# First transfers of the last stage: one fixed order on the SyncE queue, and the last left rows turned on the ScalarE queue

## The chip, the cores and the metric

The kernel runs on one core of a Trainium2 chip. The metric is the device time of one execution in microseconds. TensorE is called PE here, VectorE DVE, ScalarE ACT, GpSimd POOL and SyncE SP. SP and ACT can each issue DMA transfers on a queue of their own (q1 and q10 in the profile), and POOL issues on a third (q0). All three are served by the same 16 DMA engines.

## The reference

The reference is the forward pass and all gradients of one block: a LayerNorm, a segment-recurrent attention (32 heads of 128, 64 segments of 32 rows, each with 8 memory rows that come out of the segment before), and a dense layer with a squared ReLU beside it.

```python
def _f(x, mem0, Wq, Wk, Wv, Wo, w1, b1, w2, b2):
    xn = layernorm(x)                                  # x: [1, 2048, 512]
    return x + attention(xn, mem0, Wq, Wk, Wv, Wo) + dense(xn, w1, b1, w2, b2)

# attention, for each of 64 segments s:
h = concatenate([mem, xn[:, 32*s:32*s + 32]])          # 8 + 32 rows
q, k, v = h @ Wq, h @ Wk, h @ Wv                       # 32 heads of 128
o = (softmax(mask(q @ k.T * scale)) @ v) @ Wo
mem, out = o[:, :8], o[:, 8:]

out, vjp = jax.vjp(_f, x, mem0, Wq, Wk, Wv, Wo, w1, b1, w2, b2)
return (out, *vjp(grad_out))
```

The last stage of the kernel makes the gradients of the four attention weights, each a product over all 2560 rows (2048 rows of the segments and 512 memory rows), and finishes the gradient of x.

## The kernel before

The kernel has four stages. The first is the dense layer, forward and backward. The second walks the 64 segments forward, the third walks them backward, in blocks of four segments (`NB` = 16 blocks), with orders of operations written out by hand. The fourth (the `p5` pools) computes the weight gradients; the change is at the border of the third and the fourth stage.

**End of the third stage.** The gradients of q, k and v of the segments' rows are stored to DRAM (`S_GB`, line L1154), those of the memory rows ("left rows") of each block are turned by a transposing DMA (L1187, tile `gNat`, source `b_gkL`, `b_gvL` or `b_gqL`) and then stored to `S_GL` (L1189). Both are issued on SP's queue. `gNat` has one buffer, so the three turns of a block follow each other, each after the store of the one before. Block 0 is the last block. Its turns come after the last matmul work of the stage. The sums of a block's left rows are stored to `S_XGL` (L1182), the gradient of the segments' inputs to `S_XG` (L1192). The gradient of the first memory goes out at the very end (`gm`, L1390, stored at L1391).

**The fourth stage.** There are 16 products, in the order of `COLS`: pairs (t, g) of a weight (3 is Wo, 2 Wv, 1 Wk, 0 Wq) and a quarter of the heads. Each product is eight accumulations of 20 matmuls, 160 in all (L1503). A product has two sides:

- The gradient rows `gn` (`rows_of`, tiles `gn5` in three pools, product i uses pool i % 3, `loads(i + 2)` is called at the start of product i). For t = 3 they are plain loads of S_ON and S_OL (L1419, L1425), for the first two products on POOL's queue. For the other t they are 16 turning transfers of S_GB on SP's queue (L1422) and four plain loads of S_GL (L1425), which need the turned left rows. gn0 and gn1 are plain, gn2 is turned.
- The fixed side, `GOc` for t = 3 and `HNc` (variable `side`) for the others, made once by `slot_side`: four turning transfers (L1407) and four plain copies (L1410), on ACT's queue. A matmul needs all four turns; the copies serve the last four of the 20 rows' groups.

The results leave through `leave`: ACT copies PSUM to `wt` (L1475, six buffers), POOL issues the store (L1476). After each product, `input_rows` finishes 128 rows of the gradient of x: POOL loads XT and XL (L1444, L1446) and three more tiles (L1449 to L1453), DVE merges XL into XT (L1447), PE turns XT into `ps_rows` (L1456), and DVE, ACT and POOL do the rest.

**What sets the order.** In the third stage and wherever `tc.manual_schedule()` is open, instructions stand in the order of the Python calls. Elsewhere a planner orders them by its own costs, engine by engine. The first transfers of the fourth stage are outside of such a block before:

```python
loads(0)
slot_side(GOc, S_GM, gflat)
loads(1)
slot_side(side, S_HT, S_XN[:])
```

Of the kernel before, what the change touches and what calls it, by code (L numbers as in the profile page):

```python
# [10 lines left out]
BF16 = mybir.dt.bfloat16  # L11
F32 = mybir.dt.float32
P = 128
# [13 lines left out]
def kernel(  # L27
# [27 lines left out]
    nc = tc.nc  # L55

    _, S, D = A_x.shape
    M = A_mem0.shape[1]
# [31 lines left out]
    gflat = grad_out.flatten_outer_dims()  # L90
# [5 lines left out]
    dma = nc.sync.dma_start  # L96
# [5 lines left out]
    NB = NSEG // SPB  # L102
    HG = 4
    KH = H // HG
# [10 lines left out]
    S_XN = dram.tile([S, D], BF16, name="S_XN")  # L115
    S_GT = dram.tile([P, DC, S], BF16, name="S_GT")

    S_HT = dram.tile([P, DC, S], BF16, name="S_HT")
    S_HX = dram.tile([S // P, P, DC, P], BF16, name="S_HX")
    S_XL = dram.tile([P, DC, S // SEG * M], BF16, name="S_XL")  # L120
    S_GM = dram.tile([P, DC, S], BF16, name="S_GM")
# [19 lines left out]
    S_GL = dram.tile([NB, HG, SEG, 3, GW], BF16, name="S_GL")  # L141
# [266 lines left out]
    def turned_heads(W):  # L408

        return lambda h: W[:, :, h * P:(h + 1) * P]  # L410
# [53 lines left out]
    def turn_ops(o, alloc, R4, st):  # L464

        def tT(c):
            if "T" not in st:
                st["T"] = alloc("ps_sum")
            nc.tensor.transpose(st["T"][:, c * P:(c + 1) * P], R4()[:, c * P:(c + 1) * P], identF[:])  # L469
        for h in range(2):  # L470
            o["t%s" % "ab"[h]] = lambda h=h: [tT(c) for c in (2 * h, 2 * h + 1)]

    def left_sums(XT, T):

        for c in range(DC):
            nc.vector.tensor_reduce(XT[:, c], T[:, c * P:(c + 1) * P].rearrange("p (g j t) -> p j t g", g=HG, j=SPB),
                                    axis=AX.X, op=ALU.add)
# [145 lines left out]
    with sb("fw", 1) as fw, psum("fr", 4) as fr, psum("fpp", 1) as fpp, \  # L623
# [26 lines left out]
        def big(name):  # L650
            return fr.tile([P, 512], F32, name=name, tag="r")
# [19 lines left out]
        def block(b):  # L671

            if b not in blk:
                shapes = {"kL": (fs, [P, KH, HG, NL], BF16), "OT": (fs, [P, HG, KH, SPB, SEG], BF16),
                          "X": (fs, [P, DC, P], BF16),
                          "kM": (fo, [P, KH, HG, NL], BF16), "vTM": (fo, [P, KH, HG, NL], BF16),
                          "XT": (fs, [P, DC, SPB, SEG], F32), "qL": (fo, [P, KH, HG, NL], BF16),
                          "VL": (fo, [P, GW], BF16), "vM": (fo, [P, GW], BF16), "EL": (fo, [P, KH, KW], BF16),
                          "OTL": (fo, [P, KH, HG, NL], BF16),
                          "bb": (fo, [P, D], BF16)}  # L680

                def make(n):
                    pool, shape, dt = shapes[n]
                    return pool.tile(shape, dt, name=n, tag=n)
                blk[b] = Tiles(make)
            return blk[b]
# [250 lines left out]
    with sb("la", 2) as la, sb("ls", 2) as ls, sb("lo", 1) as lo_, sb("wg", 2) as wg, psum("lpp", 1) as lpp, psum("lr", 4) as lr:  # L937
# [84 lines left out]
        side, part = {}, {}  # L1022
# [53 lines left out]
        with tc.manual_schedule():  # L1076
# [3 lines left out]
            for b in range(NB + 1):  # L1080
                for nm in LB_ORDER:
                    k = nm.rstrip("-")
                    c = b - (nm != k)
# [23 lines left out]
    with sb("bq", 1) as bq, sb("bt", 1) as bt, sb("bs", 2) as bs, sb("be", 1) as be, psum("bpp", 1) as bpp, psum("br", 4) as br:  # L1107
# [30 lines left out]
        def left(b):  # L1138
            B_ = block(b)
            ps, st, o = {}, {}, {}  # L1140
            src = {"v": "gvL", "k": "gkL", "q": "gqL"}
            o["lq"] = lambda: dma(B_["gqL"][:], S_GQL[b])

            def following(f):

                return lambda: f(b - 1) if b > 0 else None
            for n, f in loads.items():
                o[n] = following(f)
            o["gs"] = lambda: dma(S_GM[:, :, b * P:(b + 1) * P], gts[b][:])
            for t, n in enumerate("qkv"):  # L1150
                for x in range(2):
                    def so(n=n, t=t, gs=slice(2 * x, 2 * x + 2) if n == "v" else slice(0, HG),
                           ks=slice(0, KH) if n == "v" else HALF[x]):
                        dma(S_GB[b, t][:, gs, ks], G4[n][:, gs, ks].rearrange("p g k j r -> p g k (j r)"))  # L1154
                    o["%so%d" % (n, x)] = so

            jobs = [(turned_heads(Wqkv[t]), src[n], k) for t, n in ((2, "v"), (1, "k"), (0, "q")) for k in range(KH)]
            for i in range(4):
                for x, nm in enumerate("GHI"):
                    def G_(i=i, x=x):  # L1160
                        if ("R", i) not in ps:
                            ps["R", i] = big("ps_RL")
                            ps["n", i] = 0
                        ps["n", i] += 1
                        for m, (W, n, k) in enumerate(jobs[6 * i + 2 * x:6 * i + 2 * x + 2]):
                            for g in range(HG):
                                nc.tensor.matmul(ps["R", i][32 * g:32 * g + 32, :].rearrange("p (a b) -> p a b", b=P),  # L1167
                                                 lhsT=B_[n][:, k, g, :], rhs=W(g * KH + k), start=(ps["n", i] == 1 and m == 0),
                                                 stop=(ps["n", i] == 3 and m == 1), tile_position=(0, 32 * g))
                    o["%s%d" % (nm, i)] = G_  # L1170
                if i == 0:
                    o["ra0"] = lambda: ENGS["L.ra0"](B_["R4"][:], ps["R", 0][:])
                else:
                    o["ra%d" % i] = lambda i=i: nc.vector.tensor_tensor(out=B_["R4"][:], in0=ps["R", i][:],
                                                                        in1=B_["R4"][:], op=ALU.add)
            turn_ops(o, big, lambda: B_["R4"], st)

            def xt():
                st["XL"] = bt.tile([P, DC, SPB, M], F32, name="b_XL", tag="XL")
                left_sums(st["XL"], st["T"])  # L1180
            o["xt"] = xt
            o["sl"] = lambda: dma(S_XGL[b], st["XL"][:])  # L1182

            for t, n in enumerate("qkv"):
                def nt(n=n):
                    st[n] = bt.tile([P, KH, P], BF16, name="gNat", tag="gNat")
                    nc.sync.dma_start_transpose(st[n][:], B_[src[n]][:].rearrange("p k g r -> p k (g r)"))  # L1187
                o[n + "tr"] = nt
                o[n + "st"] = lambda n=n, t=t: dma(S_GL[b].rearrange("g r t c -> (g r) t c")[:, t, :],  # L1189
                                                   st[n][:].rearrange("p k e -> p (k e)"))  # L1190

            o["sx"] = lambda: dma(S_XG[b], B_["XT"][:].rearrange("p c j r -> p c (j r)"))  # L1192
            return o

        pre, gts, loads = {}, {}, {}
# [161 lines left out]
        with tc.manual_schedule():  # L1357
# [3 lines left out]
            for b in range(NB):  # L1361
                lefts.append(left(b))
# [34 lines left out]
    with sb("p5a", 1) as p5a, sb("p5h", 1) as p5h, sb("p5", 2) as p5, sb("p5g", 1) as p5g, \  # L1397
# [6 lines left out]

        def slot_side(t_, srcT, src):
            for dc in range(DC):
                nc.scalar.dma_start_transpose(t_[:, 0:NB, dc * P:(dc + 1) * P], srcT[:, dc, :])  # L1407
            lv = src.rearrange("(c q r) d -> c q r d", q=16, r=SEG)
            for c in range(NLC):
                nc.scalar.dma_start(t_[:, NB + c, :], lv[c][:, 0:M, :])  # L1410
            return t_

        def rows_of(i, g, blocks, left_):

            t_ = (p5a, p5b, p5c)[i % 3].tile([P, RC_ALL, CW], BF16, name="gn5", tag="gn%d" % (i % 3))
            q = pdma if i < 2 else dma
            if blocks is None:
                for b in range(NB - 4, -1, -4):
                    q(t_[:, b:b + 4, :], S_ON[b:b + 4, g].rearrange("b p c -> p b c"))  # L1419
            else:  # L1420
                for b in range(NB - 1, -1, -1):
                    nc.sync.dma_start_transpose(t_[:, b, :].rearrange("p (k e) -> p k e", k=KH),  # L1422
                                                blocks(b)[:, g].rearrange("p k r -> p (k r)"))
            for j in range(SPB):
                q(t_[32 * j:32 * j + 32, NB:RC_ALL, :], left_(g).rearrange("(c j) r x -> j r c x", j=SPB)[j])  # L1425
            return t_
# [6 lines left out]
        def loads(i):  # L1433
            if i < len(COLS):
                t, g = COLS[i]
                if t == 3:
                    got[i] = rows_of(i, g, None, lambda g: S_OL[:, g])
                else:
                    got[i] = rows_of(i, g, lambda b: S_GB[b, t], lambda g: S_GL[:, g, :, t, :])
# [40 lines left out]
        p5g.tile([P, 896], BF16, name="gap5")  # L1480
        GOc = p5g.tile([P, RC_ALL, D], BF16, name="GOc")
        side = p5h.tile([P, RC_ALL, D], BF16, name="HNc")
        loads(0)
        slot_side(GOc, S_GM, gflat)
        loads(1)
        slot_side(side, S_HT, S_XN[:])
        for i, (t, g) in enumerate(COLS):
            loads(i + 2)
            gn = got[i]
# [52 lines left out]
```

## Time and profile before

| | us |
|---|---|
| median of 3 runs (lowest, highest) | 3085.69 (3084.45, 3087.76) |
| the profiled execution, its own time | 3083.57 |
| its span, first to last instruction | 3081.8 |
| PE busy in the span | 2698.1 (88%) |
| DVE, ACT, POOL busy | 1332.6, 973.0, 659.1 |
| third stage's last matmul on PE ends at | 2431.8 |
| first matmul of the fourth stage, product 0 ends | 2508.3, 2544.5 |
| last matmul of the fourth stage ends at | 3069.0 |

A line of a group gives the line of the program, the engine, the operation, the tile written and the tiles read, the count, then busy time, mean nanoseconds of one, and the idle time just before them with what ended it. Engine names with a q (SPq, ACTq, POOLq) stand for DMA issues on that engine's queue. Times of the chain and of timelines are microseconds from the start of the span. The profile is one execution; its own time is 2.1 us under the median.

### The profile page before, as it was taken

To read this page: it belongs to the slowest core of one execution; us is meant where nothing else is said; L and a number is where in the kernel's file an instruction comes from. 1 tells how busy PE (TensorE), PEld (TensorE's weight loads), DVE (VectorE), ACT (ScalarE), POOL (GpSimd) and SP (SyncE) were. 2 spreads that over 40 slices of the span, in tenths; PEclk is the share of its full clock that TensorE was granted. 3 is DMA by queue.
4 is the path that set the end of the run, shared out by engine and by line. 5 is a ranking of instruction groups with operands and counts; after the bars stand their busy time and mean duration, and the time that the engine had idled before them with its cause. 6 is when DMAs were issued, how large, how long until landed. Compare 5 with 4: busy or idle time off the path is not lost.

```text
span 3081.8 us, 109732 instructions
## 1 busy us (share of the span) xinstructions
PE 2698.1 (88%) x48600; PEld 1389.7 (45%) x48600; DVE 1332.6 (43%) x3645; ACT 973.0 (32%) x2242; POOL 659.1 (21%) x1264
## 2 busy tenths in 40 slices
PE   7997899999999886877888888888888449999998
PEld 4453444444444444455444444444444214444443
DVE  5442566666665664433454445444544201100010
ACT  2322444444444444333333333333333101111111
POOL 0000000000000000223333333333333203322222
PEclk9998999999999998998999999999999779999999
DMA  9548376867667577777567777777777879999991
GB/s 255 184 150 243 110 178 169 193 171 181 183 173 186 144 172 205 229 236 208 144 161 186 181 172 168 193 183 169 171 192 175 234 153 200 239 206 211 213 197 39
DMA packets 794558, 566.77 MB, mean 184 GB/s; under 512 B 579409, under 2 KB 681570, under 8 KB 790754
## 3 DMA queue, kind: packets, MB, share of 16 engines
q1 hardware_dynamic: 734130, 426.80, 58.7%
q0 software_dynamic: 40528, 126.53, 14.4%
q10 hardware_dynamic: 19424, 6.42, 0.9%
q8 instruction: 381, 6.24, 0.9%
q14 instruction: 95, 0.78, 0.1%
HBM read 193.61 MB, written 238.56 MB: 140 GB/s over the span
## 4 chain that ended last, share of the span: by engine, by line
PE 71%; DVE 13%; DMA 5%; issue 4%; SPq 3%; ACT 3%; POOL 1%; ACTq 0%; DVEq 0%; POOLq 0%
PE ps_gw L1503 18%; PE ps_proj L392 13%; PE ps_gR L460 9%; PE ps_R L460 4%; PE ps_L L350 3%; PE ps_sum L469 3%; PE b_pp L547 3%; PE ps_tr L165 2%; PE ps_w L1045 2%; PE ps_w L1039 2%; PE ps_RL L1167 1%; PE f_pp L547 1%; PE ps_sc L437 1%; SPq L1422 1%; PE ps_ga L279 1%
## 5 line engine op out<-in xcount | busy, mean ns | idle before, releaser
L1503 PE MATMUL ps_gw<-gn,HNc 128*128 128x512 bf16 x1920 | 416.4, 379 | 0.0
L1503 PEld LDWEIGHTS <-HNc 128*128 128x128 bf16 x1920 | 187.9, 98 | 223.8
L374 ACT CAST f_N<-ps_proj 128x512 bf16<-128x512 f32 x320 | 186.1, 582 | 243.9 <-PE ps_proj L392 228.1
L1475 ACT CAST wt<-ps_gw 128x512 bf16<-128x512 f32 x128 | 74.4, 587 | 516.1 <-PE ps_gw L1503 385.1
L392 PEld LDWEIGHTS <-X 128*32 128x32 bf16 x6144 | 153.4, 97 | 161.4 <-DVE X L482 14.1
L1458 DVE TENSOR_TENSOR gx<-ps_rows,gb 128x512 f32<-128x512 f32 x16 | 11.1, 692 | 455.3 <-PE ps_rows L1456 455.3
L1503 PE MATMUL ps_gw<-GOc,gn 128*128 128x512 bf16 x640 | 140.2, 382 | 76.5 <-DMA GOc<-S_GM 76.5
L835 POOL COPY kM<-f_kT 128x256 bf16<-128x256 bf16 x64 | 25.8, 403 | 786.2 <-DVE f_kT L377 570.3
L460 PE MATMUL ps_gR<-Wq,gq 128*32 128x512 bf16 x2048 | 149.1, 393 | 19.2 <-DVE gq L377 10.6
L374 ACT CAST gk<-b_pp 128x256 bf16<-128x256 f32 x192 | 68.9, 376 | 274.8 <-PE b_pp L547 190.9
L460 PE MATMUL ps_gR<-Wk,gk 128*32 128x512 bf16 x2048 | 144.4, 397 | 2.4 <-issue 1.7
L392 PE MATMUL ps_proj<-Wk,X 128*32 128x512 bf16 x2048 | 135.4, 384 | 12.5 <-DVE X L482 6.9
L392 PE MATMUL ps_proj<-Wo,GT 128*32 128x512 bf16 x2048 | 124.0, 384 | 14.0 <-DVE GT L482 7.3
L460 PE MATMUL ps_gR<-Wv,gv 128*32 128x512 bf16 x2048 | 135.5, 385 | 0.6 <-issue 0.5
L1503 PEld LDWEIGHTS <-gn 128*128 128x128 bf16 x640 | 62.9, 98 | 152.6 <-issue 78.8
L392 PE MATMUL ps_proj<-Wq,X 128*32 128x512 bf16 x2048 | 128.8, 382 | 0.0
L469 PE MATMUL ps_sum<-identF,R 128*128 128x128 f32 x512 | 92.6, 291 | 39.6 <-ACT R L374 35.7
L1238 POOL COPY PD<-b_P 32x320 bf16<-32x320 bf16 x256 | 115.3, 451 | 49.3 <-DMA b_P<-S_A 41.4
L1476 POOL DMA_DIRECT2D out_dram<-wt x128 | 69.4, 543 | 262.4 <-ACT wt L1475 256.5
L460 PE MATMUL ps_R<-Wo,OT 128*32 128x512 bf16 x2048 | 125.3, 385 | 0.0
L392 PE MATMUL ps_proj<-Wv,X 128*32 128x512 bf16 x2048 | 124.1, 378 | 0.0
L1251 POOL COPY b_vT<-b_vl 128x1024 bf16<-128x1024 bf16 x64 | 66.4, 1038 | 260.7 <-PE ps_sc L437 192.7
(260 smaller groups left out, 5147.9 us busy)
## 6 DMA issues: line engine op xcount, KB each, us to landing
S_A<-f_N SPq DMA_DIRECT2D x64, 512.0 KB
out_dram<-wt POOLq DMA_DIRECT2D x142, 128.0 KB, 4.9
S_A<-f_N SPq DMA_DIRECT2D x64, 256.0 KB
S_GB<-gv SPq DMA_DIRECT2D x32, 512.0 KB
S_GB<-gq SPq DMA_DIRECT2D x32, 512.0 KB
S_GB<-gk SPq DMA_DIRECT2D x32, 512.0 KB
b_kN<-S_A POOLq DMA_DIRECT2D x63, 256.0 KB, 4.4
b_qN<-S_A POOLq DMA_DIRECT2D x63, 256.0 KB, 4.2
```

Of the source, the lines that this page charges most:

```text
L165: nc.tensor.transpose(ps_ap, in_ap, ident[base:base + k, base:base + k])
L350: nc.tensor.matmul(ps[:], lhsT=x(dc), rhs=Wqkv[t][:, dc, c0:c0 + 512], start=(dc == 0), stop=(dc == DC - 1))
L374: nc.scalar.copy(out, in_)
L392: nc.tensor.matmul(o, lhsT=hT[:, dc, :], rhs=x, start=(dc == 0), stop=(dc == DC - 1), tile_position=(0, 32 * g))
L460: nc.tensor.matmul(o, lhsT=XT(k, g), rhs=x, start=(first and k == 4 * h), stop=(last and k == 4 * h + 3), tile_position=(0, 32 * g))
L469: nc.tensor.transpose(st["T"][:, c * P:(c + 1) * P], R4()[:, c * P:(c + 1) * P], identF[:])
L547: nc.tensor.matmul(o, lhsT=N_[32 * g:32 * g + m, kk * P:(kk + 1) * P], rhs=X(kk)[32 * g:32 * g + m], start=(i == 0), stop=(i == len(jobs) ...
L1238: nc.gpsimd.tensor_copy(PD[32 * g:32 * g + 32, g], C["P"][32 * g:32 * g + 32, :, 0:L])
L1251: nc.gpsimd.tensor_copy(vT[:, :, :, 0:SEG], C["vl"][:])
L1475: nc.scalar.copy(wt[:], ps[:])
L1476: pdma(dst, wt[:])
L1503: nc.tensor.matmul(ps[:], lhsT=l(rc), rhs=r(rc), start=(n == 0), stop=(n == RC_ALL - 1))
```

## The change

Three things are changed. The sides GOc and HNc are issued on SP's queue in place of ACT's. The first transfers of the stage are put into a `manual_schedule` block, which keeps the order of the calls: gn0, GOc, gn1, HNc. For the last block (b = 0), the three turns of left rows and their stores are issued on ACT's queue, and the three turned tiles get buffers of their own: k keeps `gNat`, v takes the buffer of the tag gON and q that of gOT, which the steps of the stage used before. The tag gON is also that of `gm`.

```diff
             for t, n in enumerate("qkv"):
                 def nt(n=n):
-                    st[n] = bt.tile([P, KH, P], BF16, name="gNat", tag="gNat")
-                    nc.sync.dma_start_transpose(st[n][:], B_[src[n]][:].rearrange("p k g r -> p k (g r)"))
+
+                    tag = "gNat" if b > 0 else {"k": "gNat", "v": "gON", "q": "gOT"}[n]
+                    st[n] = bt.tile([P, KH, P], BF16, name="gNat", tag=tag)
+                    (nc.sync if b > 0 else nc.scalar).dma_start_transpose(st[n][:], B_[src[n]][:].rearrange("p k g r -> p k (g r)"))
                 o[n + "tr"] = nt
-                o[n + "st"] = lambda n=n, t=t: dma(S_GL[b].rearrange("g r t c -> (g r) t c")[:, t, :],
+                o[n + "st"] = lambda n=n, t=t: (dma if b > 0 else nc.scalar.dma_start)(S_GL[b].rearrange("g r t c -> (g r) t c")[:, t, :],
                                                    st[n][:].rearrange("p k e -> p (k e)"))
...
         def slot_side(t_, srcT, src):
             for dc in range(DC):
-                nc.scalar.dma_start_transpose(t_[:, 0:NB, dc * P:(dc + 1) * P], srcT[:, dc, :])
+                nc.sync.dma_start_transpose(t_[:, 0:NB, dc * P:(dc + 1) * P], srcT[:, dc, :])
             lv = src.rearrange("(c q r) d -> c q r d", q=16, r=SEG)
             for c in range(NLC):
-                nc.scalar.dma_start(t_[:, NB + c, :], lv[c][:, 0:M, :])
+                dma(t_[:, NB + c, :], lv[c][:, 0:M, :])
             return t_
...
-        loads(0)
-        slot_side(GOc, S_GM, gflat)
-        loads(1)
-        slot_side(side, S_HT, S_XN[:])
+        with tc.manual_schedule():
+            loads(0)
+            slot_side(GOc, S_GM, gflat)
+            loads(1)
+            slot_side(side, S_HT, S_XN[:])
```

`dma` is SP's `dma_start`. In the built instructions of the changed kernel, two of the 16 turns of gn2 still stand ahead of GOc on SP's queue, since the planner orders what comes before the block; the other 14 stand behind HNc.

## The prediction

> **What bounds the kernel now.** I start with the slices and the costliest groups of the page (busy tenths in 40 slices; then busy us, mean ns | idle before, releaser).
>
> ```profile
> PE   7997899999999886877888888888888449999998
> PEclk9998999999999998998999999999999779999999
> ...
> L1503 PE MATMUL ps_gw<-gn,HNc 128*128 128x512 bf16 x1920 | 416.4, 379 | 0.0
> ...
> L1503 PE MATMUL ps_gw<-GOc,gn 128*128 128x512 bf16 x640 | 140.2, 382 | 76.5 <-DMA GOc<-S_GM 76.5
> ```
>
> PE is the bound, with one hole: slices 32 and 33. After it the last stage has no idle time at all (0.0 before 1920 matmuls), so a microsecond taken out of the hole comes off the end, unless it is given back inside the stage. The timeline of PE puts the hole at 2431.8 to 2508.3; the list of waits confirms one wait of 76.5 us for the fourth turn of GOc. The chain of waits from 2425 to 2550 (start, us, what) shows how it is filled:
>
> ```profile
> 2469.84 3.85 DMA gn<-S_GB
> ...
> 2474.33 4.47 DMA GOc<-S_GM
> 2478.82 1.23 SPq L1422
> ...
> 2480.09 3.86 DMA gn<-S_GB
> ...
> 2484.03 4.31 DMA GOc<-S_GM
> ...
> 2489.70 4.03 DMA gn<-S_GB
> ...
> 2493.81 4.77 DMA GOc<-S_GM
> ...
> 2498.60 4.14 DMA gn<-S_GB
> 2502.76 5.32 DMA GOc<-S_GM
> ```
>
> From 2474 the ACT queue's turns of GOc and the SP queue's turns of gn take turns: each waits until the other's has landed, 9.5 us for a pair, 34 us for four GOc turns. Before 2474 it is something else. The DMA view of 2432 to 2464 (packets, MB, share of 16 engines):
>
> ```profile
> q0 software_dynamic: 2668, 10.02, 92.4%
> q1 hardware_dynamic: 2730, 0.87, 12.7%
> ```
>
> POOL's loads of gn0 and gn1 (10 MB) fill the DMA engines to 2467, and a packet of 256 B on SP's queue goes only with a packet of 4 KB on POOL's: 85 a us, so a turn of 1024 packets takes some 12 us (two issues of L1422 lasted 10.7 and 14.9). From 2468 to 2472, with POOL's loads done, q1 alone moved 2733 packets in 4 us.
>
> **What the Trainium skill says.** *DMA: Bandwidth & Descriptors*, section "DMA Transpose (X-bar)": the first transpose of a later stream has to wait for the full completion of the other stream's. The trace agrees: no turn of one queue was issued before the other's had landed. Same page, "Queues, rings and completion order": each DMA engine goes round its queues packet by packet; agrees (2668 against 2730). *TensorE: Matmul & The Clock Gate*, Part 1: after idling, PE runs at half rate until about 3.4 us of work. Agrees: a clock of 0.50 in the hole, and the first product lasted 36.16 us, the second 34.70.
>
> **The change, part by part.** What follows is read from the order of the built instructions of both kernels, engine by engine, and from what each waits for; times are of the trace before.
>
> *1. Order on POOL.* Before, POOL's first load is a piece of gn1, which waits for PE (2428.5), and gn0 stands behind it. Now gn0's eight loads stand first; their last wait is the second S_GB<-gv store, landed at 2420.4. They start 8 us earlier. But DMA was at 0.61 from 2420 to 2428 and 0.91 to 2432: only some 3.5 us of it was free. POOL's end moves from 2467 to about 2462 to 2463. PE's own last load (b_gqL) landed at 2419.2, so I cost PE before 2431.8 at nothing; without that cover, some 1 to 3 us.
>
> *2. Turns of the last left rows (L1187, now on ACT).* k is issued at 2426.7, behind ACT's last copy (before: 2428.3), its S_GL store when k has landed, then v. On ACT nothing is queued behind until the copy L1475 at the end of product 0, so ACT costs nothing. But SP's first gn turn now waits for v, and all of SP's queue (S_XGL, GOc, HNc) is behind it. Estimate from the packet rates: POOL's mean packet is 0.924 x 35 us x 16 / 2668 = 0.19 us; k's 64 packets on each engine share with POOL's and the S_GB stores' (0.05 us each), 64 x 0.265 = 17 us from 2428; store and issue 3 us; v shares with POOL, 63 x 0.217 = 14 us, then its rest. v lands at about 2461 (bounds 2450, with POOL's start as slow as the 3.7 us from its issue to its first packet before, and 2466).
>
> *3. Sides on SP.* After v: two gn turns (1.25 us of issue each, they stayed in front), then GOc 1, 4.5 us from its issue: 2461 + 2.6 + 4.5 = 2468. Then q on ACT, which waits for GOc 1: 3.6 us (2488.4 to 2491.9 before), 2472. GOc 2, which waits for q: 4.5, 2476.5. GOc 3 and 4 follow on the same queue without a wait: 2.75 each (HNc 3 and 4 stood 2.5 and 2.8 apart), 2482.2. The two switches that are left cost 8 us; before there were seven. Product 0 needs gn0 (landed long before), GOc 1 to 4 and the bank of gm; gm (L1390) now waits for v's store because v's tile has its tag, near 2464: hidden. Bounds: if v is early, POOL's loads hold up the gn turns instead, 2478; if v lands at 2466 and the switches take 5.3, 2491. Gain 26 us (17 to 30).
>
> *4. What SP has to do beside.* Eight turns and eight copies more, all ahead of the other 14 gn turns of gn2. HNc 4 x 2.75 + 8 copies x 0.62 ends at 2498, 14 turns x 1.8 (29 us for 16 in later products) at 2524, S_GL at 2530. Product 2 begins after 2550: hidden. gn3 then waits for SP some 5 us, takes 44 as before (2544.5 to 2588), 2570, and is due near 2600: hidden, 30 us left.
>
> *5. The order on POOL after product 0.* This is given back. Before, XT and XL, which `ps_rows` needs, are loaded long ahead; the second pair comes after the stores:
>
> ```profile
> 2492.47 0.56 POOL L1444 DMA_DIRECT2D XT<-S_XG  x1 [39.21 <-DMA gNat<-b_gqL]
> 2493.02 0.56 POOL L1446 DMA_DIRECT2D XL<-S_XGL  x1
> ```
>
> ```profile
> 2544.49 2.68 POOL L1476 DMA_DIRECT2D out_dram<-wt  x5
> 2550.56 0.54 POOL L1476 DMA_DIRECT2D out_dram<-wt  x1 [3.39 <-issue]
> ...
> 2552.27 0.58 POOL L1476 DMA_DIRECT2D out_dram<-wt  x1
> 2552.85 0.54 POOL L1444 DMA_DIRECT2D XT<-S_XG  x1
> 2553.39 0.54 POOL L1446 DMA_DIRECT2D XL<-S_XGL  x1
> ```
>
> ```profile
> 2561.35 0.23 DVE L1447 COPY XT<-XL 128x128 f32<-128x128 f32 x1 [6.64 <-DMA XL<-S_XGL]
> ```
>
> In the new order the first XT and XL stand behind the eight out_dram stores of product 0, which wait for the copies L1475, which wait for product 0. On PE `ps_rows` (L1456) still stands directly after the product's last matmul, so PE waits. Let E be product 0's end (2544.5 before). Store 7 needs its copy, which waits for store 1 to land (E + 2.9, 0.6 long); store 8 at E + 4.0, XT at E + 4.6, XL at E + 5.1. Low: XL lands 2.6 later, as the first did: PE resumes at E + 8. High: with the 3.4 us of "issue" ahead of store 7 and the 7.8 us that the second XL took beside SP's turns: E + 16. I take E + 12, since gn3's turns start at E as before. After such a hole PE starts at half clock: in two earlier gaps of 12 and 9 us the granted clock fell to 0.5 and stayed there for 4 to 5 us; 36.16 - 34.70 = 1.5 us (0 to 2).
>
> **Sum.** -26 + 12 + 1.5 = -12.5 us. Against the profiled execution, 3083.57 (span 3081.8 and 1.8 around it), 3071.1. The median of the runs, 3085.69, is 2.1 higher; I carry the difference over: 3073.2. Ends: -30 + 8 = -22, and -17 + 16 + 2 = +1.
>
> **The rivals.**
> - *Given back whole* (0.14): the hole ends at 2488 or later and the wait for XT takes its upper bound. -20 + 16 + 1.5 = -2.5, 3083. For it: the landing of XL beside SP's turns was 7.8 us; against: the stores alone are not that long.
> - *Full gain* (0.08): XT is served before the stores' copies, or `ps_rows` doesn't hold PE. -26, 3059.7. Against: the order of POOL and PE, both fixed.
> - *Slower: the turns crawl* (0.10). k, its store, v, in series behind POOL's 10 MB, with all of SP waiting for v. Hole's end = v + 21.2; break-even is 2508.3 - 13.5 = 2494.8, so it decides where v lands at 2473.6 or later. At 2483: 2504.2 + 13.5 = +9.4, 3095. For it: a turn beside POOL's loads took up to 14.9 us, and two are in series from 2427; against: POOL's loads end by 2467 and the rest of a turn then runs in 2 us.
> - That the change doesn't do what it says is part of the forecast: the sides aren't ahead of all gradient rows (two gn turns stayed in front), and q's turn stands between GOc 1 and 2.
>
> **How the numbers follow.** 0.2% is 6.2 us, about what a measurement of this kernel can tell from no change. The forecast has 0.68, nearly all of it beyond -6.2; with the full gain, 0.76 faster. Same 0.14, slower 0.10. The range holds the forecast's ends and most of the same case: 3073.2 - 10 = 3063 to 3085; the full gain and the crawl are left out.
>
> **What would show it.** Step 1: gn<-S_ON issued near 2420 and ended by 2463. Step 2: gNat<-b_gvL landing near 2461, ahead of any gn turn. Step 3: in the chain, GOc four times with one switch to ACT between the first and second, and PE's first ps_gw near 2482. Step 5: a new idle of 8 to 16 us before ps_rows, released by DVE's XT, and a second stretch of half clock. Wrong if that idle is absent, if the first ps_gw comes after 2495, or if PE waits for gn or HNc later in the stage.

## The result, and the profile after

In the first comparison the changed kernel took 3083.52 us (median of 4 runs, 3076.88 to 3086.24) and the kernel before 3085.07: a ratio of 0.9992, 95% interval 0.9973 to 1.0011. Two later comparisons of the same two kernels, on which more below, gave 0.9962 (0.9948 to 0.9976) and 0.9980 (0.9964 to 0.9996). The forecast, 3073.2 over 3085.69, is 0.9960: the second comparison alone fits it, the first can't be told from no change. So the change is worth a few microseconds of 3085, some 7 by the mean of the three ratios and some 3 by the three traces below, and the forecast of 12.5 was too large by both. The execution shown here took 3081.8 us, with a span of 3080.0.

The page of the changed kernel, slices and groups (busy tenths; then busy us, mean ns | idle before, releaser). Three lines were added above this place, so L1503 is now L1506:

```profile
PE   7997899999999886877898888888888549999998
PEclk9998999999999998988999999999999879999999
...
L1506 PE MATMUL ps_gw<-gn,HNc 128*128 128x512 bf16 x1920 | 416.4, 379 | 0.0
...
L1506 PE MATMUL ps_gw<-GOc,gn 128*128 128x512 bf16 x640 | 141.7, 385 | 55.7 <-DMA GOc<-S_GM 55.7
```

The hole in front of the last stage went from 76.5 us to 55.7: slices 32 and 33 went from 44 to 54, and in the row of the clock from 77 to 87. The matmuls that follow are as busy as before (416.4), and the end of the span moved by 1.8 us only. The list of waits of PE over the border shows what the page's groups don't, a second wait that the kernel before didn't have:

```profile
PE ps_gw L1506 <- DMA GOc<-S_GM: 55.7, 1, 55.7
PE ps_rows L1458 <- DVE XT L1449: 15.7, 1, 15.7
```

The chain of waits (start, us, what) shows the new order at work. The turns of k and v stand in series, the gn turns wait for v, and GOc changes queues once, for q:

```profile
2428.07 21.31 DMA gNat<-b_gkL
...
2449.45 0.35 ACTq L1191
...
2449.84 16.76 DMA gNat<-b_gvL
...
2466.66 1.31 SPq L1424
...
2468.02 1.88 SPq L1424
...
2470.26 4.55 DMA GOc<-S_GM
...
2474.96 3.03 DMA gNat<-b_gqL
...
2478.05 2.92 SPq L1409
...
2481.55 2.36 SPq L1409
...
2483.96 2.63 SPq L1409
```

PE's first matmul follows at 2488.86. Product 0 ends at 2525.5, and the timelines of ACT, POOL and DVE show why PE then stands still:

```profile
2531.22 0.59 ACT L1477 CAST wt<-ps_gw 128x512 bf16<-128x512 f32 x1 [4.12 <-DMA out_dram<-wt]
```

```profile
2524.95 3.26 POOL L1478 DMA_DIRECT2D out_dram<-wt  x6 [75.76 <-ACT wt L1477]
2532.10 0.54 POOL L1478 DMA_DIRECT2D out_dram<-wt  x1 [3.90 <-ACT wt L1477]
2533.34 0.54 POOL L1478 DMA_DIRECT2D out_dram<-wt  x1 [0.69 <-ACT wt L1477]
2534.06 0.54 POOL L1446 DMA_DIRECT2D XT<-S_XG  x1 [0.18 <-issue]
2534.60 0.54 POOL L1448 DMA_DIRECT2D XL<-S_XGL  x1
```

```profile
2540.92 0.26 DVE L1449 COPY XT<-XL 128x128 f32<-128x128 f32 x1 [70.14 <-DMA gn<-S_GB]
```

XT and XL are issued behind eight stores, 8.5 us after the product's end; the seventh of these is late because ACT's copy for it waited 4.12 us for an earlier store to land. The copy that merges XT and XL starts 6.3 us after XL's issue. Its line names a gn turn as what ended its wait; of the transfers whose data it needs, XT and XL are the last. Before, they had been loaded in the hole.

**A measure that doesn't scatter.** The third stage's last matmul ended between 2417.8 and 2456.8 us in the 14 traces of this study, although that stage's work is nearly the same in all; two traces of the kernel before alone have 2431.8 and 2442.2. That is where most of the scatter of the traces sits. Part of it is a difference between the comparisons: the kernel before had a median of 3095.09 us beside c2, c3 and f5, but 3085.70 beside e1, e2, e3 and e9, 3083.83 beside c1, e4, e10 and f3, and 3083.96 beside f6. So a time is read against its own comparison, by the ratio. What the edits touch comes after the third stage's end: the hole, and the time from the hole's end to the last matmul (that of the last `ps_rows`, at 3069.5 before). In the kernel before these are 76.6 + 561.1 = 637.7 in one trace and 76.9 + 561.3 = 638.2 in the other. Ahead of the third stage's end the change moves only gn0's loads and k's turn, and PE lost nothing by that: from the same `ps_gR` group, at 2403.81 us before and at 2405.22 after, to that end it is 28.0 us in both. All kernels, in this measure and by their runs (us; the last column but one is 1 plus the difference over 3085):

| kernel | hole | from there to the end | together | against 637.7 | ratio from this | ratio measured (95%) |
|---|---|---|---|---|---|---|
| changed, first trace | 55.7 | 579.0 | 634.7 | -3.0 | 0.9990 | 0.9992 (0.9973 to 1.0011) |
| changed, second (c1) | 53.8 | 583.1 | 636.9 | -0.8 | 0.9997 | 0.9962 (0.9948 to 0.9976) |
| changed, third (c3) | 53.8 | 579.1 | 632.9 | -4.8 | 0.9984 | 0.9980 (0.9964 to 0.9996) |
| XT early (e1) | 51.1 | 562.3 | 613.4 | -24.3 | 0.9921 | 0.9904 (0.9870 to 0.9937) |
| turns undone (e3) | 59.5 | 561.2 | 620.7 | -17.0 | 0.9945 | 0.9938 (0.9915 to 0.9961) |
| turns on SP (e2) | 45.2 | 578.7 | 623.9 | -13.8 | 0.9955 | 0.9942 (0.9916 to 0.9967) |
| XT early, gn1 on SP (e9) | 45.5 | 561.6 | 607.1 | -30.6 | 0.9901 | 0.9904 (0.9876 to 0.9931) |
| turns alone (e4) | 81.7 | 576.7 | 658.4 | +20.7 | 1.0067 | 1.0055 (1.0037 to 1.0073) |
| XT early, turns on SP (e10) | 46.5 | 561.4 | 607.9 | -29.8 | 0.9903 | 0.9912 (0.9887 to 0.9938) |
| e10, gn1 on SP last (f3) | 41.0 | 562.5 | 603.5 | -34.2 | 0.9889 | 0.9893 (0.9858 to 0.9928) |
| f3, rows on SP (f5) | 34.8 | 569.1 | 603.9 | -33.8 | 0.9890 | 0.9887 (0.9869 to 0.9905) |
| f5, gn2 first (f6) | 29.7 | 567.5 | 597.2 | -40.5 | 0.9869 | 0.9864 (0.9847 to 0.9880) |

The ratio from the trace lies within the measured interval for every kernel but one, the second trace of the changed kernel. The measure leaves out what follows the last matmul: 12.2 to 12.3 us in ten of the traces, but 15.7 in e9 and f3 and 14.6 in f5 and f6, which would raise their ratios from the trace by about 0.001 and leaves them inside. The third column has two groups, 561 to 563 where XT comes early or the turns are undone, and 577 to 583 where XT waits behind the stores; f5 and f6 lie between, since each has another short wait.

### The profile page after: what moved, and what is told of

Its sections match the earlier page's. It is cut to its first block, busy times and chain, and to the rows that moved or that the text cites. A ratio compares the mean times of both kernels' runs of the same rounds, so it can differ in the third digit from the quotient of the medians.

```text
span 3080.0 us, 109732 instructions
## 1 busy us (share of the span) xinstructions
PE 2697.4 (88%) x48600; PEld 1388.1 (45%) x48600; DVE 1332.2 (43%) x3645; ACT 973.3 (32%) x2242; POOL 659.4 (21%) x1264
## 5 line engine op out<-in xcount | busy, mean ns | idle before, releaser
L1506 PE MATMUL ps_gw<-gn,HNc 128*128 128x512 bf16 x1920 | 416.4, 379 | 0.0
L1506 PEld LDWEIGHTS <-HNc 128*128 128x128 bf16 x1920 | 187.8, 98 | 223.9
L1506 PE MATMUL ps_gw<-GOc,gn 128*128 128x512 bf16 x640 | 141.7, 385 | 55.7 <-DMA GOc<-S_GM 55.7
L392 PE MATMUL ps_proj<-Wk,X 128*32 128x512 bf16 x2048 | 135.0, 384 | 12.6 <-DVE X L482 6.9
L1506 PEld LDWEIGHTS <-gn 128*128 128x128 bf16 x640 | 63.4, 99 | 132.8 <-issue 59.9
```

The source lines that it names most:

```text
L392: nc.tensor.matmul(o, lhsT=hT[:, dc, :], rhs=x, start=(dc == 0), stop=(dc == DC - 1), tile_position=(0, 32 * g))
L1506: nc.tensor.matmul(ps[:], lhsT=l(rc), rhs=r(rc), start=(n == 0), stop=(n == RC_ALL - 1))
```

## The experiments

My theory after the result: the hole shrank as forecast in kind, and 17.9 us (579.0 - 561.1) were given back by XT and XL behind product 0's stores. The rivals were that PE would be held there by something else as well, or that the hole had only moved.

### XT early (e1)

```diff
-        def input_rows(b):
+        early = {}
+        def x_rows(b):
             XT = p5.tile([P, DC, P], F32, name="XT5", tag="XT5")
             pdma(XT[:], S_XG[b])
             XL = p5.tile([P, DC, SPB, M], F32, name="XL5", tag="XL5")
             pdma(XL[:], S_XGL[b])
+            early[b] = XT, XL
+        def input_rows(b):
+            if b not in early:
+                x_rows(b)
+            XT, XL = early[b]
...
             slot_side(side, S_HT, S_XN[:])
+            x_rows(NB - 1)
```

> The changed kernel with the loads of the first input_rows (XT and XL alone) issued inside the fixed order, behind HNc, so that on POOL they stand ahead of product 0's eight stores. Theory A (the gain of 20.8 us in the hole is given back by XT and XL standing behind the stores): the hole stays at 55 to 57 us, the idle time before ps_rows goes from 15.7 to under 1 us, the second stretch of half clock goes, and the time is 15 to 18 us under the changed kernel's: 3066 to 3068, ratio to the kernel before 0.994 to 0.995. Rival B (PE would be held at that place by something else too, by gb behind the stores or by a PSUM bank): an idle time of 8 us or more stays before ps_rows or before product 1, and the time is within 6 us of the changed kernel's. Rival C (two more loads beside the turns lengthen the hole): the hole is 60 us or more.

Measured: no wait before ps_rows, 3060.19 us, ratio 0.9904 (0.9870 to 0.9937), better than the 0.994 to 0.995 expected. In the list of waits of PE over the border one of the two is left:

```profile
PE ps_gw L1514 <- DMA GOc<-S_GM: 51.1, 1, 51.1
```

Rivals B and C fall. From the hole's end to the end it is 562.3 us and not 579.0: 16.7 us of the 17.9 come back by two loads that stand elsewhere in a queue. The hole itself was 51.1 us, under the 55 to 57 expected; v's turn took 14.15 us here and 15.9 to 16.8 in the three traces of the changed kernel. Nothing in the edit reaches v, so I put down only 16.7 us to the edit; why the hole was shorter in this trace stays open.

### The turns undone (e3), the turns alone (e4)

e3 is the changed kernel with the old lines for the turns and their stores, on SP with one `gNat`; e4 is the kernel before with the new lines for both, and nothing else. The turns' lines of e3:

```diff
-                    tag = "gNat" if b > 0 else {"k": "gNat", "v": "gON", "q": "gOT"}[n]
-                    st[n] = bt.tile([P, KH, P], BF16, name="gNat", tag=tag)
-                    (nc.sync if b > 0 else nc.scalar).dma_start_transpose(st[n][:], B_[src[n]][:].rearrange("p k g r -> p k (g r)"))
+                    st[n] = bt.tile([P, KH, P], BF16, name="gNat", tag="gNat")
+                    nc.sync.dma_start_transpose(st[n][:], B_[src[n]][:].rearrange("p k g r -> p k (g r)"))
```

> The changed kernel with the part of the turns undone: one gNat tile, turns and stores of the last left rows on the SyncE queue as before; sides on SyncE and the fixed order stay. On POOL, XT and XL then stand ahead of product 0's stores again. Theory A (the order of the sides is the gain; the turns on ScalarE bring only the wait for XT, and hold SyncE's queue to the landing of v): GOc's first turn is issued near 2472 after the six gn turns beside POOL's loads, q's after it on the same queue, first ps_gw 2482 to 2486, no idle time before ps_rows, 3056 to 3063 us, ratio 0.990 to 0.993. Rival B (the turns on ScalarE make most of the shorter hole): the hole is 65 us or longer, and the time 3070 us or more. Rival C (the wait for XT does not come from the turns): the idle time of 12 to 17 us before ps_rows stays.

Measured for e3: hole 59.5 us, no wait before ps_rows, 3066.13 us, ratio 0.9938 (0.9915 to 0.9961). The hole lies between what theory A and rival B named. The chain says what A missed: with one tile, each turn waits for the store of the one before to land.

```profile
2453.52 4.45 DMA S_GL<-gNat
...
2457.99 1.79 SPq L1187
...
2462.59 4.26 DMA S_GL<-gNat
...
2466.86 1.25 SPq L1187
...
2468.48 1.82 SPq L1407
```

These two landings are 8.7 us; without them, and if nothing else took their place, the hole would be some 50.8, an estimate. The three tiles alone, with the stores left on SP, were not tried. The wait for XT is gone, so it is part of the price of the turns' edit: rival C falls.

> The kernel before with the part of the turns alone: k, v and q in three tiles on the ScalarE queue, the sides still on ScalarE, no fixed order. Theory A (the turns on ScalarE shorten nothing by themselves, because the sides still change queues with the gn turns, and they push XT and XL behind product 0's stores): hole 70 to 77 us, 13 to 17 us idle before ps_rows, from the hole's end to the end some 578 us and not 561; 3092 to 3103 us, ratio 1.002 to 1.006. Rival B (the turns on ScalarE shorten the hole by themselves): hole under 65 us. Rival C (XT falls behind the stores because of the fixed order, not of the turns): no idle time before ps_rows, 3080 to 3087 us.

Measured for e4: hole 81.7 us, 12.1 us idle before ps_rows, 3099.06 us, ratio 1.0055 (1.0037 to 1.0073): slower. Slower here means that the interval lies above 1. Theory A holds in kind, with an idle time a microsecond under its 13 to 17, and rivals B and C fall. The hole is even some 5 us longer than A said; the piece up to the first GOc turn takes 47.0 us from the third stage's end (2426.7 to 2473.69) and not 42.5 (2431.8 to 2474.33). After it the chain is the old alternation, a gn turn on SP and a GOc turn on ACT each waiting for the other:

```profile
2473.69 4.47 DMA GOc<-S_GM
...
2479.99 4.16 DMA gn<-S_GB
2484.23 4.42 DMA GOc<-S_GM
...
2489.99 3.85 DMA gn<-S_GB
2493.90 4.49 DMA GOc<-S_GM
```

So the two halves of the change have opposite signs. The sides on SP in a fixed order save 17.0 us by themselves (e3); the queue and the order were not tried apart. The turns' edit costs 20.7 by itself (e4), and 14.0 on top of the sides (-17.0 to -3.0).

### The turns on SP (e2)

The three tiles stay, and the turns go back to SP's queue; the stores stay on ACT.

```diff
-                    (nc.sync if b > 0 else nc.scalar).dma_start_transpose(st[n][:], B_[src[n]][:].rearrange("p k g r -> p k (g r)"))
+                    nc.sync.dma_start_transpose(st[n][:], B_[src[n]][:].rearrange("p k g r -> p k (g r)"))
```

> The changed kernel with the three tiles kept, but the three turns issued on SyncE (their stores stay on ScalarE): k, v and q stand in a row ahead of the gn turns and GOc. Theory A (v is late because two turns stand in series behind a landing and a store each, at POOL's packet rate, and q adds two switches of the queue): k, v and q are 3072 packets at some 85 a us beside POOL, done by 2466; one gn turn, GOc 1 to 4 without a switch; first ps_gw 2478 to 2484, hole 45 to 51; XT still stands behind the stores on POOL, so the idle time of 14 to 17 us before ps_rows stays; 3073 to 3079 us. Rival B (POOL's loads alone set when the turns end, whichever queue they are on): first ps_gw 2487 to 2491 as in the changed kernel, 3081 to 3085 us.

Measured: hole 45.2 us, 13.8 us idle before ps_rows, 3067.03 us, ratio 0.9942 (0.9916 to 0.9967). Its first ps_gw came at 2463.1, but its third stage ended early, at 2417.8; the hole is the number to compare, and it lies at the short end of 45 to 51. The time is some 6 us under the expected 3073 to 3079; the trace, with 13.8 us under the kernel before, makes it 3072. Theory A holds on the hole and on the wait: three turns in a row on one queue, with no store and no landing between, are over sooner than two in series on another.

```profile
2414.40 13.32 SPq L1189
...
2428.44 11.64 SPq L1189
...
2440.17 7.20 SPq L1189
...
2447.47 1.26 SPq L1424
...
2449.08 3.03 SPq L1409
```

The wait for XT stays although ACT turns nothing here. It comes with the three tiles or with the stores on ACT, through the planner's order; which of the two was not tried.

### gn1 off POOL (e9), and both mends (e10)

e9 is e1 with gn1's loads on SP, between GOc and HNc. e10 is e1 and e2 together.

```diff
-            q = pdma if i < 2 else dma
+            q = pdma if i < 1 else dma
```

> As the kernel with XT and XL early, and gn1's loads moved from POOL to SyncE, between GOc and HNc, so that 5 MB and not 10 run beside the turns of k and v. Theory A (the turns crawl at the packet rate of POOL's loads, so with half of these v lands earlier): POOL's loads end near 2446, k lands by 2449, v by 2456, first ps_gw 2474 to 2480, hole 41 to 47, no idle time before ps_rows; 3052 to 3060 us, ratio 0.989 to 0.992. Rival B (the loads on POOL do not set it): hole 53 us or more, time as the kernel with XT and XL early. Rival C (gn1 now lands too late): PE waits for gn before product 1 or for HNc before the first HNc product.

Measured: hole 45.5 us, no wait before ps_rows, 3059.75 us, ratio 0.9904 (0.9876 to 0.9931). The chain:

```profile
2430.47 17.15 DMA gNat<-b_gkL
...
2448.09 3.13 DMA gNat<-b_gvL
...
2468.20 12.61 DMA GOc<-S_GM
```

With POOL's loads over at 2446, v's turn takes 3.13 us instead of 16.76: what made it long is the traffic beside it. But 8 us of this went again in GOc's fourth turn, 12.6 us instead of the 4.8 of e1, which no theory had. I read it at first as the effect of gn1's loads behind it on the same queue; f3 and f5 below show another cause that is enough by itself.

> Both single mends together: XT and XL early in the fixed order, and the three turns on SyncE. Theory A (they are independent: one is a wait after product 0, the other the length of the hole): hole 44 to 49 us, no idle time before ps_rows, 561 us from the hole's end to the end; against the kernel before 76.5 - 46 = 30 us, 3053 to 3058 us, ratio 0.989 to 0.992. Rival B (with XT early the later turns or gn2 become late): PE waits for gn or HNc later in the stage, and the time is 3060 us or more.

Measured: hole 46.5 us, 561.4 us from there to the end, no second wait, 3056.62 us, ratio 0.9912 (0.9887 to 0.9938). The trace has theory A on every point: the hole of e2 and the rest of e1, so the two mends are independent there. The runs alone don't show it, since e10's interval and e1's (0.9870 to 0.9937) overlap.

### Nothing beside the turns (f3, f5), and gn2 in time (f6)

f3 is e10 with gn1's loads on SP (the line of e9), behind HNc.

```diff
             slot_side(GOc, S_GM, gflat)
-            loads(1)
             slot_side(side, S_HT, S_XN[:])
+            loads(1)
```

> As the kernel with both mends, and gn1's loads on SyncE behind HNc, so that neither POOL's queue nor GOc's turns share the DMA engines with them. Theory A (5 MB less beside the turns: with gn1 off POOL v's turn lasted 3.1 us and not 14 to 17, and the last GOc turn took 12.6 us only because gn1's loads stood right behind it): k, v and q done 16 to 24 us after the third stage's last matmul, hole 30 to 40 us, GOc 4 landing within 5 us of its issue; gn1 lands some 35 us after GOc, so PE waits 0 to 6 us before product 1; 3044 to 3054 us, ratio 0.986 to 0.990. Rival B (gn1 is late): 8 us or more of idle time before product 1, and no better than 3058 us.

Measured: hole 41.0 us, no wait for gn1, 3052.43 us, ratio 0.9893 (0.9858 to 0.9928). Better than e10 by the trace (the intervals overlap), but a microsecond past the range for the hole, and GOc's fourth turn was slow again although gn1, issued from 2488, now stands far behind. The chain:

```profile
2447.83 6.97 DMA S_GL<-gNat
...
2462.14 13.47 DMA GOc<-S_GM
```

Its first line is v's store, which the gm tile waits for and which was hidden in the changed kernel: here it is on the chain, and in f5 again (7.3 us). POOL's timeline shows what ran beside the fourth turn: with gn1 gone from its queue, the planner moved ten loads of the input rows there. The first eight of them:

```profile
2456.11 0.56 POOL L1447 DMA_DIRECT2D XT<-S_XG  x1 [28.54 <-DVE gm L1392]
2456.66 0.55 POOL L1449 DMA_DIRECT2D XL<-S_XGL  x1
2457.33 0.54 POOL L1458 DMA_DIRECT2D gb<-S_GXNB  x1
2457.86 0.54 POOL L1460 DMA_DIRECT2D xn<-S_XN  x1
2458.39 0.54 POOL L1462 DMA_DIRECT2D gi<-in_grad_out_dram  x1
2458.92 0.54 POOL L1447 DMA_DIRECT2D XT<-S_XG  x1
2459.44 0.54 POOL L1449 DMA_DIRECT2D XL<-S_XGL  x1
2459.97 0.54 POOL L1458 DMA_DIRECT2D gb<-S_GXNB  x1
```

f5 takes these away from POOL. They are issued on SP in the fixed order, XT and XL of the first rows ahead of gn1, the rest behind it.

```diff
             slot_side(side, S_HT, S_XN[:])
+            first = x_rows(NB - 1, dma)
             loads(1)
-            x_rows(NB - 1)
+            early[NB - 1] = first + g_rows(NB - 1, dma)
+            early[NB - 2] = x_rows(NB - 2, dma) + g_rows(NB - 2, dma)
```

`x_rows` and `g_rows` are the loads of `input_rows`, XT and XL in the one and gb, xn and gi in the other, on the queue that is named.

> Turns of k, v and q on SyncE, and behind HNc on the same queue XT and XL of the first input rows, gn1, and the other loads of the first two input rows: nothing of 4 KB packets is left on POOL's queue between gn0 and product 0's stores. Theory A (in the kernel with gn1 last GOc's fourth turn took 13.5 us, against 4.6 to 4.8 in three others, because ten loads of the input rows on POOL ran beside it): GOc 4 lands within 6 us of its issue, hole 30 to 35 us, no idle time before ps_rows or product 1; 3043 to 3050 us, ratio 0.986 to 0.989. Rival B (the fourth turn was slow because of what stands behind it on its own queue): it takes 10 us or more again, hole 39 to 43 us. Rival C (gn1, now later and with 1.6 MB more on its queue, is late): 3 us or more of idle time before product 1.

Measured: GOc's fourth turn had landed by 4.8 us after its issue (issued at 2468.99, first ps_gw at 2473.81), hole 34.8 us, 3058.14 us, ratio 0.9887 (0.9869 to 0.9905). The time is past the expected 3043 to 3050 because the kernel before was slower in this comparison too; the ratio is in the range. Theory A holds on the hole: without the ten loads the turn is short, and in f3 it was long with gn1 far away, so these loads are enough to make it long. In e9 both were there, the ten loads from 2465.89 and gn1's from 2475.45, and gn1's share in its 12.6 us was not told apart. How the loads do it stays open too: from 2466 to 2470 in f3 only 521 packets moved, 154 GB/s, under half of the 336 that the changed kernel moved from 2428 to 2450. But the kernel is no better than f3 together, because a new wait takes the gain, for gn2 and not for gn1 as rival C had it (list of waits of PE):

```profile
PE ps_gw L1517 <- DMA GOc<-S_GM: 34.8, 1, 34.8
PE ps_gw L1517 <- DMA gn<-S_GL: 4.5, 1, 4.5
```

f6 calls `loads(2)` inside the fixed order as well, and no longer at the start of product 0.

```diff
             loads(1)
+            loads(2)
             early[NB - 1] = first + g_rows(NB - 1, dma)
...
-            loads(i + 2)
+            if i > 0:
+                loads(i + 2)
```

> As the kernel with the rows on SyncE, and gn2's loads inside the fixed order too, behind gn1 and ahead of the gb, xn and gi loads. Theory A (there PE waited 4.5 us for gn2 because 1.6 MB of rows, 13.6 us of the queue, stood ahead of its turns): no idle time for gn before product 2, hole 33 to 36 us (one gn turn less ahead of GOc), 561 to 563 us from the hole's end to the end; 76.7 - 34.5 = 42 us under the kernel before, ratio 0.985 to 0.988. Rival B (gn2 is late because of gn1's 5 MB, or the rows that now land late take its place): an idle time of 3 us or more before product 2, before ps_rows or for a bank of PSUM, and no more than 36 us saved.

Measured: hole 29.7 us, no wait for gn, 3042.70 us, ratio 0.9864 (0.9847 to 0.9880): the best kernel of the study, some 42 us (1.36% of 3085) under the kernel before. The hole is shorter than theory A had it. Part of rival B is there, the rows that now land late, but more than its 36 us was saved:

```profile
PE ps_gw L1519 <- DMA GOc<-S_GM: 29.7, 1, 29.7
PE ps_rows L1466 <- ACT n L1475: 3.6, 1, 3.6
```

### The controls (c1, c2, c3)

c1 and c3 are the changed kernel again, c2 the kernel before against its own runs.

> The changed kernel itself, as a control beside the others on their chip. Every theory: a hole of 51 to 57 us, 14 to 17 us idle before ps_rows, 3079 to 3086 us, ratio to the kernel before 0.998 to 1.0. What it tells: how far the hole itself moves from one execution to the next, since the kernel with XT early had 51.1 us with the same turns.

> The kernel before itself, as a control: a second trace of it, and its time against its own runs. Every theory: ratio 1.0 within its interval. The theory of the last stage (a kernel's time is the end of the third stage's last matmul, plus the hole, plus what follows it; only the last two differ between the kernels) expects a hole of 74 to 79 us and 561 to 562 us from the hole's end to the last matmul, so 636 to 640 us together, and all of the scatter in the third stage's end, which was 2431.8 us in the first trace. Rival (the hole itself scatters as the times do): the two together are more than 5 us from 637.7.

> The changed kernel again beside the kernel before, with more rounds: the two comparisons so far, 0.9992 (0.9973 to 1.0011) and 0.9962 (0.9948 to 0.9976), differ. The balance of the last stage (hole 53.8 to 55.7 us, then 579 to 583 us to the end, against 637.7 together before) expects 1 to 3 us saved, ratio 0.999 to 1.0. Rival (something ahead of the last stage also became faster): ratio 0.995 to 0.997, and a third stage that ends 5 us or more earlier than the control's in the kernel before.

Measured: c2 1.0000 (0.9985 to 1.0016), hole 76.9 us and 561.3 after it, together 638.2: the sum repeats within 0.5 us while the third stage ended 10.4 us later, as the theory of the last stage said. For c1 the waits were 53.8 and 18.2 us and the ratio 0.9962 (0.9948 to 0.9976), all but the hole outside what every theory expected; for c3 53.8 and 14.0 us and 0.9980 (0.9964 to 0.9996). c3's third stage ended at 2456.8 us, later than the control's 2442.2, but its trace is of the slowest of its 14 executions (3103.82 us), so this says little of a gain ahead of the last stage. c1's ended 4.2 us earlier than the first trace of the kernel before, and had that lead at the same `ps_gR` group already, 28.0 us ahead of the third stage's end, ahead of every transfer that the change moved. The three traces give 0.8 to 4.8 us, the three ratios 2.5 to 11.7. Why the ratios give more than the traces stays open: no trace shows a gain ahead of the last stage, but each is one execution.

## Why the prediction was right and wrong

The mechanism was right in each step, the place of what is given back included, but for one piece of step 5. The sizes of two terms were not, both on the side of the loss, and with them what a measurement can see: "faster by over 0.2%" was forecast at 0.76, and the rival *given back whole*, which took the upper ends of the same two terms, is nearest to what came. From the trace: -20.9 for the hole and +17.9 after it, -3.0, where the forecast had -26 + 13.5 = -12.5 and that rival -2.5.

1. *POOL.* gn0 was issued at 2422.45 and the last packet of POOL's loads started at 2465.8. The forecast said near 2420 and 2462 to 2463; allowing 1.4 us for the later end of the third stage, the start was a microsecond out and the end 1.4 to 2.4.
2. *The turns on ACT: the first mis-sized term.* v was to land at 2461, 29.2 us after the third stage's end; it landed at 2466.6, 33.4 after it: 4.2 us too late. One of these was a slip in the sum: 2428 and 17, 3 and 14 us make 2462. The rest is the time between the packets. k's first packet came 3.9 us after its issue, where the sum had 1.3 (2426.7 to 2428). From k's last packet to v's first 6.7 us passed, k's store standing in between on the same queue, and I had 3 for store and issue; from v's last packet to its landing 0.6, which had no number. The packets were priced well for k, whose 1024 ran from 2431.99 to 2448.4, 16.4 us against 17. For v, from 2455.1 to 2466.0, they took 10.9 against 14, and that was luck: it hid 3 us of what was missing. The price of 0.19 us for a packet of POOL was also come by wrongly, since 2668 packets belong to 32 us and not to 35; the same sum with 32 gives 0.18. The DMA view of 2428 to 2450 shows the traffic (packets, MB, share of 16 engines):

```profile
q0 software_dynamic: 1546, 5.76, 79.7%
q1 hardware_dynamic: 1338, 1.37, 19.3%
q10 hardware_dynamic: 1056, 0.26, 5.8%
```

   From 2434 to 2436 the three queues moved 148, 155 and 149 packets. The Trainium skill (*DMA: Bandwidth & Descriptors*, "Queues, rings and completion order") says that each engine goes round its queues; the trace agrees, with 1 to 1 to 1 as the share in this stretch, though their bytes differ (0.57, 0.19 and 0.04 MB). While k's packets ran, from 2432 to 2448.4, it was 1058, 1038 and 1039; while v's ran, POOL moved only 629 beside ACT's 1065, and why it moved fewer is not shown. e9 shows the other end: with POOL quiet, v's first packet came 1.2 us after its issue.
3. *GOc on SP.* From v's landing to the first ps_gw 22.3 us against 21.2: right. 4.2 + 1.1 is the whole of what the hole missed (20.9 against 26). gm's wait for v's store was hidden, as said; in f3 and f5, where the turns came earlier, it was not.
4. *SP's additional work* was hidden, as said: PE waited for neither gn nor HNc in the changed kernel. In f5, with gn1 and the rows on SP besides, that cover was used up.
5. *XT behind the stores: right in kind, the second mis-sized term.* 15.7 us against 12 (8 to 16). Let E be product 0's end, 2525.5. XT was issued at E + 8.5, where the low case had E + 4.6, and the copy came 6.3 us after XL's issue, where it had 2.6. The high case came near, but its first piece was another one: the 3.4 us of "issue" ahead of store 7. What came is the landing of a store. The copy for store 7 waits for it, was to start at E + 2.9 and started at E + 5.7, after a wait of 4.12 us for `out_dram<-wt`. So the upper end was reached partly by luck. The middle had been taken without a reason in the profile, with XL's 7.8 us beside SP's turns in the rows shown of product 1 before. The clock took what is left of the 17.9 after the wait, 2.1 us, against 1.5; product 0, which was not in that term, has 0.5 of it. The granted clock was 0.66 in the wait and 0.70 in the 4.7 us after it.

*The turns crawl*, which decided from a landing of v at 2473.6, was 8.4 us away (2473.6 is 2475.0 with the shift of 1.4): v landed 0.8 us after POOL's last packet started, which fits its counter-argument that the end of POOL's loads bounds it. *Full gain* had no part in the changed kernel; e1 is what it looks like once the order of POOL is mended.

## What to carry to other kernels

Moving loads off one queue lets a planner reorder another: look where the loads of the next small step went, because two late loads of 0.3 MB cost 16.7 us here, more than all that the turns on a third queue brought. Price a small transfer beside a heavy one in three pieces: issue to first packet, packets at the share that the trace shows (one for one with each busy queue here, while both had work), and whatever stands ahead of it on its own queue; and where an estimate's two bounds both come from rows of the trace, ask which of the rows has the same transfers beside it before taking the middle. When a kernel's runs scatter by more than the effect, measure from the last point that the edit can't reach.

## What the runs showed of the hardware that I had not expected

- Beside POOL's loads a turning transfer on an otherwise empty queue took 3.9 us to its first packet (k), and 1.2 us when they were over (v in e9, right behind k's store).
- Ten loads of input rows on POOL's queue, 1.7 MB together, were enough to slow a turn: GOc's fourth took 13.5 us beside them in f3 and 12.6 in e9 (there with gn1's loads behind it too), against 4.6 to 4.8 in c1, e1, e10 and f5.
- The stretch from the first matmul of the last stage to its last repeated within 0.2 us in two executions of the kernel before that differed by 10.9 us as a whole (3083.57 and 3094.5, from comparisons whose medians of the kernel before are 3085 and 3095).
